# Top-k attention with a mixture of depths on one core: an exponential per head, bounds checked at the end, and the mixture's matmuls placed behind the turning of scores

## The chip, the core and the metric

One of the eight cores of a Trainium2 chip runs the whole program. The metric is the device time of one execution in microseconds (us). A core has engines that each work through a list of instructions in order: TensorE (PE in the profile, its weight loads PEld), VectorE (DVE), ScalarE (ACT), GpSimd (POOL), and SyncE (SP), which here only issues DMAs. They wait for one another through semaphores. PSUM, where TensorE writes, has banks of 512 f32 values per partition.

## What is computed

Batch 8, 8 heads, 576 positions, head dimension 64; every score row keeps its 32 largest entries.

```python
scores = scale * np.matmul(q, k.transpose(0, 1, 3, 2))
kth = np.partition(scores, -32, axis=-1)[..., -32:-31]
scores = np.where(scores >= kth, scores, -1e9)
attn = np.exp(scores - max);  attn = attn / (attn.sum(-1) + 1e-9)
x = (attn @ v) as (8, 576, 512)
# mixture of depths, for each batch b
s = x[b] @ w_gate
idx = the 128 positions of the largest s
out[b] = x[b];  out[b, idx] += sigmoid(s[idx]) * (relu(x[b, idx] @ w1) @ w2)
```

## The kernel before

The attention is cut into **units**: one pair of heads by one tile of 128 query rows (two pairs and the last 64 rows in the last tile). A batch has 18 units (`per_batch`), and there are `N` = 144. A unit passes through a pipeline that is written out by hand as one loop over steps `n`; the class `InOrder` keeps every engine's instructions in exactly the program's order. Nothing is planned by a scheduler. A unit m goes through these steps:

- `multiply` and `keep`: TensorE multiplies q by k into the PSUM tile `ps`, ScalarE copies it to `sc` (step m-1).
- `find_bound`: VectorE takes the eight largest of seven parts of each row (`cand`), then three rounds (`best`, `bound`) give a lower bound for the 32nd largest score (step m).
- `what_is_below`: ScalarE takes the sign of score minus bound (`sides`, counting into `seen`), GpSimd multiplies scores by signs into `y` (two instructions, one for each head) and `fill` adds a few values (step m+1).
- `kth_of`: VectorE finds the exact 32nd score (`next8`) as the eighth largest of `y` (step m+2).
- `mask_of`: `less` marks what is below it; head 0 on ScalarE, head 1 on GpSimd (step m+3).
- `weigh`, `values`, `keep_values`: TensorE transposes the scores and adds a large negative number where `less` is set (`turn`, into the PSUM tile `ptr`; one more 128 x 128 block, `turn_last`, goes to a corner of the bank `av`). ScalarE takes the exponential of both heads in one instruction (`pT`, 1024 columns from two banks) and of the corner (`last`). TensorE multiplies `pT` by v into `av`, and ScalarE copies the result to `xs` (step m+4).

Between these the program puts small work in by queues that are emptied at fixed points of a step: `late` (ScalarE, by `flush()` right after the mask), `vector_late` (VectorE, between the two heads of `find_bound`) and `pool_late` (GpSimd). A finished row tile is divided by its sums (`rden` on VectorE, `x` on GpSimd) and dotted with the gate weights (`prod` on VectorE).

The **mixture** of batch b runs while batch b+1 and the first half of b+2 are in the loop, cut into 25 pieces by a generator; `mix_steps` says after which step a piece comes. The first pieces store and reload the gates and count ranks; later ones fetch 128 rows, transpose them, and do one eighth of the first product (`multiply_h`, four matmuls into `h_ps`) or of the second (`y_ps`, one matmul). In the kernel before, the pieces of step n are issued at the very end of step n, so that on TensorE they stand behind `values` and ahead of the next step's `turn`.

`keep_least` is called once for each batch, behind `mask_of` of its last unit. On VectorE it takes the low 23 bits of all 36 bounds of the batch (`low`), and three minima into `least`: of the bounds, of the 32nd scores, and of `low`. At the end of the program these minima, `seen`, `sums`, `ranks` and `others` are reduced to one number per partition, `sure`; `count_unsure` sums it over partitions by a matmul on TensorE, and a general version of everything runs if a case was found that the fast way does not cover. It did not run here.

The last batch's mixture, `closing`, cannot hide behind other units. Its order on TensorE is: the rest of the y matmuls of the batch before (`between`), the transposes of the fetched rows `xe`, the matmul of `count_unsure`, then four blocks of `multiply_h` and the 8 matmuls of the second product.

Of the kernel before, what the change touches and what calls it, by code (L numbers as in the profile page):

```python
# [10 lines left out]
AF = mybir.ActivationFunctionType  # L11
# [20 lines left out]
J = 4  # L32
# [16 lines left out]
def kernel(  # L49
# [80 lines left out]

    NS = B * 2 * (J * NHP + NHP // 2)
    seen = const.tile([P, NS], FP32, name="seen")
    least = const.tile([P, 3, B], FP32, name="least")
    sums = const.tile([P, B * NT, H], FP32, name="sums")
    nc.gpsimd.memset(sums, 1.0)

# [50 lines left out]
    def flush():  # L187
        while late:
            late.pop(0)()
# [119 lines left out]
                    )  # L309

    def turn_pair(rows, hp, copy=None):
        tr = ps_tr.tile([P, 2, J, P], FP32, name="ptr")
        for w in range(2):
            rows.turn(2 * hp + w, tr[:, w, :, :])
        for w in range(2):
            rows.keep(2 * hp + w, tr[:, w, :, :], copy=copy)

    def turn_all_last(rows, copy=None):
        tr = ps_misc.tile([P, 2, 2, P], FP32, name="tr", tag="misc")
# [149 lines left out]
    def turn_some(tr, z, less):  # L469

        pe.transpose(tr, z, ident)
        if less is not None:
            pe.matmul(
                tr, less, out_of_reach, start=False, stop=True, skip_group_check=True
            )

    def room_to_turn():
        return ps_tr.tile([P, 2, J, P], FP32, name="ptr"), ps_av.tile(
            [P, 512], FP32, name="av"
        )  # L480

    def turn(z, tr, less=None):

        for i in range(2):
            for c in range(J):
                at = slice(c * P + i * R, (c + 1) * P + i * R)
                turn_some(
                    tr[:, i, c, :], z[:, i, at], None if less is None else less[:, i, at]
                )

    def turn_last(z, av, less=None):
# [11 lines left out]
    def values(t, g, pT, last, av, vs):  # L503

        vt, vpair = vs
        for i, heads in enumerate(heads_of(t, g)):
            for c in range(J):
                for r in (0, R):
                    h = heads[-1 if r else 0][0]
                    pe.matmul(
                        av[r : r + R, i * DE : (i + 1) * DE],
                        pT[:, i, c, r : r + R],
                        vt[:, h, c, :],
                        start=(c == 0 and i == 0),  # L520
                        stop=False,
                        skip_group_check=True,
                    )
# [222 lines left out]
    def closing(b, pg, between):  # L746
# [7 lines left out]
        pick = modpool.tile([P, NT, CAP], BF16, name="pick")  # L754

        def spread(t0, t1):
            tr = ps_tr.tile([P, 2, J, P], FP32, name="ptr")
            n = R if t0 == J else P
            for t in range(t0, t1):
                pe.transpose(  # L760
                    tr[:, 0, t - t0, 0:n],
                    gate[0:n, t : t + 1].to_broadcast([n, P]),
                    ident[0:n, 0:n],
                )
            act.copy(
                out=gate_row[:, t0 * P : (t1 - 1) * P + n].rearrange(
                    "p (t i) -> p t i", i=n
                ),
                in_=tr[:, 0, 0 : t1 - t0, 0:n],
            )  # L770

        def count(t, among, rank):
# [59 lines left out]
        dve.reciprocal(out=g, in_=g)  # L832

        xeT = modpool.tile([P, NDC, CAP], FP32, name="xeT")
        ps = ps_tr.tile([P, 2, J, P], FP32, name="ptr")[:, 0, :, :]
# [5 lines left out]
        for f0 in range(0, NFC, 2):  # L841
            h_ps = (
                lambda: room_for_scores()[:, 0, 0, :],
                lambda: ps_av.tile([P, 512], FP32, name="av"),
                lambda: ps_misc.tile([P, 512], FP32, name="h_ps", tag="misc"),
                lambda: ps_tr.tile([P, 2, J, P], FP32, name="ptr")[:, 0, :, :].rearrange(
                    "p c i -> p (c i)"
                ),
            )[f0 // 2 % 4]()
# [183 lines left out]
    def is_unit(n):  # L1033
        return 0 <= n < N

    def weigh(sc, tr, av, less):

        turn(sc, tr, less)
        tr_last = turn_last(sc, av, less)
        pT = ptpool.tile([P, 2, J, P], FP32, name="pT")  # L1040
        last = ptpool.tile([P, P], FP32, name="last")

        def exp():
            act.activation(pT, tr, AF.Exp, scale=scale)
            act.activation(last, tr_last, AF.Exp, scale=scale)

        return pT, last, exp
# [23 lines left out]
        find_kth(ys.pop(n), next8s[b][:, i, :, :])  # L1071

    def keep_least(b, bound, kth):
        low = stats.tile([P, per_batch, 2], I32, name="low", bufs=1)
        dve.tensor_scalar(
            out=low,
            in0=bound.bitcast(I32),
            scalar1=(1 << 23) - 1,
            scalar2=1,
            op0=ALU.bitwise_and,  # L1080
            op1=ALU.bitwise_xor,
        )
        for w, of in enumerate((bound, kth, low)):
            dve.tensor_reduce(
                out=least[:, w, b : b + 1], in_=of, axis=mybir.AxisListType.XY, op=ALU.min
            )

    def mask_of(n, on=None):
        b, i = divmod(n, per_batch)
        masks[n] = mask(scs[n], next8s[b][:, i, :, :], on)  # L1090
        if i == per_batch - 1 and b < B - 1:
            keep_least(b, bounds.pop(b)[:, :, :, 7], next8s.pop(b)[:, :, :, 7])

    for n in range(-1, N):
        b, i = divmod(n, per_batch)
# [25 lines left out]
        if is_unit(n - 4):  # L1121
            tr, av = room_to_turn()
            pT, last, exp = weigh(scs.pop(n - 4), tr, av, masks.pop(n - 4))
            exp()
        if is_unit(n - 3):
            mask_of(n - 3, (act, None) if n in scatter_steps else None)
        flush()
# [47 lines left out]
        if gating is not None:  # L1175
            b, t = gating
            if t == J:
                store(out[b], of_batch[b][0])
                mixtures[b] = mixture(float(b * S), of_batch[b][1], ranks[:, b, :])
        for b in mix_steps.get(n, ()):  # L1180
            next(mixtures[b], None)
        b, i = divmod(n, per_batch)
        if i == v_at and 0 <= b < B - 1:
            load_v(v[b + 1], qkv[b + 1][2])
# [2 lines left out]

    def other_room():
        ps = room_for_scores()
        return ps[:, 0, :, :].rearrange("p u (c i) -> p u c i", c=J), ps[:, 1, 0, :]  # L1190

    x, pg = of_batch[B - 1]
    between = mixtures[B - 2]
# [16 lines left out]
    def sums_of(t, xs):  # L1210
        n = R if t == J else P
        keep_sums(n, xs, sums[0:n, (B - 1) * NT + t, :])

    weigh_unit(N - 4)
    weighed[N - 4][2]()
    what_is_below(N - 1)
# [36 lines left out]


    keep_least(B - 1, bounds.pop(B - 1)[:, :, :, 7], next8s.pop(B - 1)[:, :, :, 7])
    sure = stats.tile([P, 1], FP32, name="sure")
    dve.memset(sure, 1.0)
    for what, op, than, limit in (
        (least[:, 0, :], ALU.min, ALU.is_gt, LEAST),
        (least[:, 1, :], ALU.min, ALU.is_gt, LEAST),  # L1260
        (least[:, 2, :], ALU.min, ALU.is_gt, 0.5),
        (seen, ALU.max, ALU.is_lt, float(MIDDLE)),
        (seen, ALU.min, ALU.is_gt, float(MIDDLE - 16)),
        (sums.rearrange("p t h -> p (t h)"), ALU.min, ALU.is_gt, FEWEST),
        (sums.rearrange("p t h -> p (t h)"), ALU.max, ALU.is_lt, MOST),
    ):
# [62 lines left out]
    def general(b, row0):  # L1329
# [11 lines left out]
        for t in range(NT):  # L1341
            xs = xpool.tile([P, H, DE], FP32, name="xs")
            for g in range(groups(t)):
                ps = room_for_scores()
                multiply(t, g, kT, qT, ps)
                p = general_weights(keep(ps))
                tr, av = room_to_turn()
                turn(p, tr)
                pT = ptpool.tile([P, 2, J, P], FP32, name="pT")
                last = ptpool.tile([P, P], FP32, name="last")  # L1350
                nc.scalar.copy(out=pT, in_=tr)
# [53 lines left out]
```

## Time and profile before

| | |
|---|---|
| median of 3 runs | 827.2 us (826.03 to 827.62) |
| the profiled execution: its own time, its span | 828.44 us, 826.1 us |
| VectorE busy | 787.2 us (95%) |
| TensorE busy | 777.0 us (94%) |
| ScalarE busy | 730.7 us (88%) |
| GpSimd busy | 715.4 us (87%) |
| mean granted TensorE clock | 0.990 |

The span runs from the first to the last instruction; all times inside the profile are counted from its start. Busy time is the union of an engine's instruction intervals, and neighbouring instructions overlap a little: a row's duration is longer than the distance from its start to the next start. In a group of instructions the columns are engine, operation, output<-inputs, shapes, count, then busy time and mean duration in nanoseconds, then the idle time before them and what ended it. Almost all instructions carry line 45, where `InOrder` records them, so they are told apart by tile names.

### The profile page before, as it was taken

The page shows a single profiled execution, that of the slowest core. Times are in us where ns is not written, and L with a number is a line of the kernel's source. Part 1 is how long each engine was busy: PE and PEld are TensorE (multiplying, and loading weights), DVE is VectorE, ACT ScalarE, POOL GpSimd, SP SyncE. Part 2 cuts the span into 40 slices and gives each one's busy share as a digit, 9 for nine tenths or more (in the row PEclk, how much of TensorE's full clock was granted, in tenths as well). Part 3 has the DMA queues.
Part 4 walks back from the last instruction along what each step waited for, and adds up shares of the span by engine and source line. Part 5 has one row for each costly group of instructions (what it writes and reads, how often), then busy time and mean ns, then how long its engine had stood idle before and what let it go on. Part 6 is the DMA issues. An engine that isn't in the chain of part 4 may idle for free. (4 is left out here: it accounts for less than half of the span.)

```text
span 826.1 us, 28252 instructions
## 1 busy us (share of the span) xinstructions
PE 777.0 (94%) x10143; PEld 596.5 (72%) x10143; DVE 787.2 (95%) x4651; ACT 730.7 (88%) x1557; POOL 715.4 (87%) x722
## 2 busy tenths in 40 slices
PE   6888888888999999999999999999999999999976
PEld 5566666666887778877787777877787777767744
DVE  7899999999999999999999999999999999999960
ACT  4799999999999999999999999999999999879831
POOL 3799999999899999999899999999999998899831
PEclk9699999999999999999999999999999999999999
DMA  7931111521141221521223221512215102101021
GB/s 170 283 86 40 28 66 28 105 53 27 60 92 36 53 40 59 112 47 34 79 47 86 53 40 60 104 23 54 40 59 112 28 15 66 23 12 18 2 71 30
DMA packets 122133, 50.38 MB, mean 61 GB/s; under 512 B 116417, under 2 KB 116417, under 8 KB 120961
## 3 DMA queue, kind: packets, MB, share of 16 engines
q1 hardware_dynamic: 118672, 43.91, 22.0%
q0 software_dynamic: 1728, 4.20, 2.8%
q8 instruction: 82, 1.34, 0.8%
q14 instruction: 67, 0.54, 0.3%
q10 hardware_dynamic: 1584, 0.39, 0.2%
HBM read 36.93 MB, written 11.55 MB: 59 GB/s over the span
## 5 line engine op out<-in xcount | busy, mean ns | idle before, releaser
L45 POOL TENSOR_TENSOR y<-sc,sides 128x576 f32<-128x576 f32 x288 | 365.1, 1289 | 57.0 <-ACT sides L45 54.3
L45 DVE MAX8 cand<-sc 128x8 f32<-128x82 f32 (+1 forms) x2016 | 314.0, 228 | 2.7 <-ACT sc L45 2.7
L45 POOL TENSOR_SCALAR less<-sc,next 128x576 bf16<-128x576 f32 x135 | 232.5, 1722 | 12.9 <-DVE next L45 10.0
L45 PE MATMUL ptr<-out_of_reach,less 128*128 128x128 bf16 x1136 | 205.3, 220 | 19.5 <-POOL less L45 19.4
L45 ACT ACTIVATE sides<-sc,bound 128x576 bf16<-128x576 f32 x288 | 223.0, 787 | 0.0
L45 PE MATMUL ptr<-ident,sc 128*128 128x128 f32 x1136 | 217.0, 282 | 0.0
L45 DVE MAX8 next<-y 128x8 f32<-128x584 f32 x288 | 204.4, 751 | 1.7 <-POOL y L45 1.6
L45 PEld LDWEIGHTS av<-v,pT 128*64 128x64 f32 x4544 | 144.1, 137 | 66.9 <-ACT last L45 63.2
L45 PE MATMUL ps<-kT,qT 64*128 64x288 f32 (+1 forms) x1280 | 182.0, 431 | 5.2 <-ACT qT L45 5.2
L45 PEld LDWEIGHTS ptr<-ident,sc 128*128 128x128 f32 x1136 | 161.3, 142 | 29.1 <-issue 17.4
L45 ACT ACTIVATE pT<-ptr 128x1024 f32<-128x1024 f32 x142 | 145.3, 1023 | 33.2 <-PE ptr L45 32.2
L45 PE MATMUL av<-v,pT 128*64 128x65 f32 x4544 | 163.7, 224 | 9.3 <-ACT last L45 8.5
L45 ACT COPY sc<-ps 128x1152 f32<-128x1152 f32 (+1 forms) x144 | 162.2, 1126 | 3.5 <-PE ps L45 3.5
L45 PEld LDWEIGHTS <-less 128*128 128x128 bf16 x1296 | 136.1, 106 | 39.2 <-POOL less L45 25.2
L45 PEld LDWEIGHTS ps<-kT,qT 64*128 64x128 f32 (+1 forms) x1280 | 100.2, 178 | 41.5 <-issue 21.2
L45 ACT ACTIVATE less<-sc,next 128x576 bf16<-128x576 f32 x143 | 111.2, 777 | 12.7 <-DVE next L45 10.8
L45 DVE MATCH_REPLACE8 cand<-best,cand 128x21 f32<-128x21 f32 (+1 forms) x576 | 99.0, 180 | 0.0
L45 DVE MAX8 best<-cand 128x8 f32<-128x21 f32 (+1 forms) x576 | 90.5, 190 | 0.0
L45 PE MATMUL h_ps<-xeT,w 128*128 128x128 f32 x464 | 65.8, 286 | 0.0
L45 PEld LDWEIGHTS h_ps<-xeT,w 128*128 128x128 f32 x464 | 55.8, 191 | 9.2 <-issue 5.8
L45 PE MATMUL y_ps<-w,hT 128*128 128x512 f32 x112 | 60.6, 636 | 0.0
L45 ACT ACTIVATION_READ_ACCUMULATOR sides<-sc,bound 128x1 f32 x288 | 59.9, 208 | 0.0
(133 smaller groups left out, 866.4 us busy)
## 6 DMA issues: line engine op xcount, KB each, us to landing
v<-in_v_dram SPq DMA_DIRECT2D x64, 128.0 KB, 4.2
out_dram<-x SPq DMA_DIRECT2D x8, 1024.0 KB, 3.9
rows<-in_k_dram SPq DMA_DIRECT2D x56, 128.0 KB, 2.9
rows<-in_q_dram SPq DMA_DIRECT2D x56, 128.0 KB, 3.1
w<-in_moe_w_dram SPq DMA_DIRECT2D x2, 2048.0 KB
gate_row<-row_dram SPq DMA_DIRECT2D x7, 288.0 KB, 4.4
w<-in_k_dram SPq DMA_DIRECT2D x8, 128.0 KB, 3.2
last<-in_k_dram SPq DMA_DIRECT2D x8, 128.0 KB, 4.0
```

What stands on the lines that cost most here:

```text
L45: return lambda *a, **kw: self._tc.keep_in_program_order(fn(*a, **kw))
```

## The change

1. **A bank and an exponential for each head.** The two-bank tile `ptr` becomes two one-bank tiles, and `pT` two tiles. The exponential of a unit is issued as two instructions of 512 columns, one for each head, and then `last` as before. The same one-bank tiles serve the turning of k and q at the start and the closing mixture.
2. **The bounds' bits at the end.** `keep_least` no longer forms `low` and two of its minima. ScalarE copies the 36 bounds of a batch to `bounded` (through `late`), and VectorE keeps only the minimum of the 32nd scores. At the end `low` is formed over all 288 bounds at once, and `bounded` and `low` are reduced there, ahead of `count_unsure`.
3. **The mixture's pieces one place later.** The pieces of step n are issued in step n+1, behind the turning and the exponentials and ahead of the mask. On TensorE they stand between `turn` and `multiply`. Side by side, the instruction lists of SP and GpSimd are the same in both kernels, apart from names; on VectorE only the instructions of item 2 and the order of a few small ones differ.

```diff
     def turn_pair(rows, hp, copy=None):
-        tr = ps_tr.tile([P, 2, J, P], FP32, name="ptr")
+        tr = [turn_bank(w) for w in range(2)]
         for w in range(2):
-            rows.turn(2 * hp + w, tr[:, w, :, :])
+            rows.turn(2 * hp + w, tr[w])
...
+    def turn_bank(i=0):
+        return ps_tr.tile([P, J, P], FP32, name=f"ptr{i}")
...
+    def room_for_weights():
+        return [ptpool.tile([P, J, P], FP32, name=f"pT{i}") for i in range(2)], ptpool.tile(
+            [P, P], FP32, name="last"
         )
...
         def exp():
-            act.activation(pT, tr, AF.Exp, scale=scale)
+            for i in range(2):
+                act.activation(pT[i], tr[i], AF.Exp, scale=scale)
             act.activation(last, tr_last, AF.Exp, scale=scale)
...
     def keep_least(b, bound, kth):
-        low = stats.tile([P, per_batch, 2], I32, name="low", bufs=1)
-        dve.tensor_scalar(
-            out=low,
-            in0=bound.bitcast(I32),
-            scalar1=(1 << 23) - 1,
-            scalar2=1,
-            op0=ALU.bitwise_and,
-            op1=ALU.bitwise_xor,
-        )
-        for w, of in enumerate((bound, kth, low)):
-            dve.tensor_reduce(
-                out=least[:, w, b : b + 1], in_=of, axis=mybir.AxisListType.XY, op=ALU.min
-            )
+        at = 2 * per_batch * b
+        late.append(
+            lambda: act.copy(
+                out=bounded[:, at : at + 2 * per_batch].rearrange("p (n i) -> p n i", i=2),
+                in_=bound,
+            )
+        )
+        dve.tensor_reduce(
+            out=least[:, b : b + 1], in_=kth, axis=mybir.AxisListType.XY, op=ALU.min
+        )
...
+    def mix(n):
+        for b in mix_steps.get(n, ()):
+            next(mixtures[b], None)
...
             pT, last, exp = weigh(scs.pop(n - 4), tr, av, masks.pop(n - 4))
             exp()
+        mix(n - 1)
         if is_unit(n - 3):
             mask_of(n - 3, (act, None) if n in scatter_steps else None)
         flush()
...
-        for b in mix_steps.get(n, ()):
-            next(mixtures[b], None)
...
+    mix(N - 1)
     weigh_unit(N - 4)
...
     keep_least(B - 1, bounds.pop(B - 1)[:, :, :, 7], next8s.pop(B - 1)[:, :, :, 7])
+    flush()
+    low = modpool.tile([P, S], I32, name="low", tag="scratch")[:, 0:NS]
+    dve.tensor_scalar(
+        out=low,
+        in0=bounded.bitcast(I32),
+        scalar1=(1 << 23) - 1,
+        scalar2=1,
+        op0=ALU.bitwise_and,
+        op1=ALU.bitwise_xor,
+    )
     for what, op, than, limit in (
-        (least[:, 0, :], ALU.min, ALU.is_gt, LEAST),
-        (least[:, 1, :], ALU.min, ALU.is_gt, LEAST),
-        (least[:, 2, :], ALU.min, ALU.is_gt, 0.5),
+        (bounded, ALU.min, ALU.is_gt, LEAST),
+        (least, ALU.min, ALU.is_gt, LEAST),
+        (low, ALU.min, ALU.is_gt, 0.5),
```

More of the change, by code (lines that the diff above doesn't have):

```diff
@@ L132 @@
     seen = const.tile([P, NS], FP32, name="seen")
-    least = const.tile([P, 3, B], FP32, name="least")
+    least = const.tile([P, B], FP32, name="least")
+    bounded = const.tile([P, NS], FP32, name="bounded")
     sums = const.tile([P, B * NT, H], FP32, name="sums")
@@ L311, in turn_pair @@
     def turn_pair(rows, hp, copy=None):
-        tr = ps_tr.tile([P, 2, J, P], FP32, name="ptr")
+        tr = [turn_bank(w) for w in range(2)]
         for w in range(2):
-            rows.turn(2 * hp + w, tr[:, w, :, :])
+            rows.turn(2 * hp + w, tr[w])
         for w in range(2):
-            rows.keep(2 * hp + w, tr[:, w, :, :], copy=copy)
+            rows.keep(2 * hp + w, tr[w], copy=copy)
     def turn_all_last(rows, copy=None):
@@ L475, in turn_some @@
             )
+    def turn_bank(i=0):
+        return ps_tr.tile([P, J, P], FP32, name=f"ptr{i}")
     def room_to_turn():
-        return ps_tr.tile([P, 2, J, P], FP32, name="ptr"), ps_av.tile(
-            [P, 512], FP32, name="av"
+        return [turn_bank(i) for i in range(2)], ps_av.tile([P, 512], FP32, name="av")
+    def room_for_weights():
+        return [ptpool.tile([P, J, P], FP32, name=f"pT{i}") for i in range(2)], ptpool.tile(
+            [P, P], FP32, name="last"
         )
@@ L487, in turn @@
                 turn_some(
-                    tr[:, i, c, :], z[:, i, at], None if less is None else less[:, i, at]
+                    tr[i][:, c, :], z[:, i, at], None if less is None else less[:, i, at]
                 )
@@ L517, in values @@
                         av[r : r + R, i * DE : (i + 1) * DE],
-                        pT[:, i, c, r : r + R],
+                        pT[i][:, c, r : r + R],
                         vt[:, h, c, :],
@@ L756, in spread @@
         def spread(t0, t1):
-            tr = ps_tr.tile([P, 2, J, P], FP32, name="ptr")
+            tr = turn_bank()
             n = R if t0 == J else P
@@ L760, in spread @@
                 pe.transpose(
-                    tr[:, 0, t - t0, 0:n],
+                    tr[:, t - t0, 0:n],
                     gate[0:n, t : t + 1].to_broadcast([n, P]),
@@ L768, in spread @@
                 ),
-                in_=tr[:, 0, 0 : t1 - t0, 0:n],
+                in_=tr[:, 0 : t1 - t0, 0:n],
             )
@@ L834, in closing @@
         xeT = modpool.tile([P, NDC, CAP], FP32, name="xeT")
-        ps = ps_tr.tile([P, 2, J, P], FP32, name="ptr")[:, 0, :, :]
+        ps = turn_bank()
         for dc in range(NDC):
@@ L845, in closing @@
                 lambda: ps_misc.tile([P, 512], FP32, name="h_ps", tag="misc"),
-                lambda: ps_tr.tile([P, 2, J, P], FP32, name="ptr")[:, 0, :, :].rearrange(
-                    "p c i -> p (c i)"
-                ),
+                lambda: turn_bank().rearrange("p c i -> p (c i)"),
             )[f0 // 2 % 4]()
@@ L1039, in weigh @@
         tr_last = turn_last(sc, av, less)
-        pT = ptpool.tile([P, 2, J, P], FP32, name="pT")
-        last = ptpool.tile([P, P], FP32, name="last")
+        pT, last = room_for_weights()
         def exp():
-            act.activation(pT, tr, AF.Exp, scale=scale)
+            for i in range(2):
+                act.activation(pT[i], tr[i], AF.Exp, scale=scale)
             act.activation(last, tr_last, AF.Exp, scale=scale)
@@ L1189, in other_room @@
         ps = room_for_scores()
-        return ps[:, 0, :, :].rearrange("p u (c i) -> p u c i", c=J), ps[:, 1, 0, :]
+        banks = [ps[:, 0, i, :].rearrange("p (c i) -> p c i", c=J) for i in range(2)]
+        return banks, ps[:, 1, 0, :]
     x, pg = of_batch[B - 1]
@@ L1348, in general @@
                 turn(p, tr)
-                pT = ptpool.tile([P, 2, J, P], FP32, name="pT")
-                last = ptpool.tile([P, P], FP32, name="last")
-                nc.scalar.copy(out=pT, in_=tr)
+                pT, last = room_for_weights()
+                for i in range(2):
+                    nc.scalar.copy(out=pT[i], in_=tr[i])
                 nc.scalar.copy(out=last, in_=turn_last(p, av))
```

## The prediction, made before the changed kernel ran

> **What bounds the kernel now.** I read the busy times first, then the stages in windows, then the list of waits, and last the timeline around the instructions that the change touches. The page's first line does not decide:
>
> ```profile
> PE 777.0 (94%) x10143; PEld 596.5 (72%) x10143; DVE 787.2 (95%) x4651; ACT 730.7 (88%) x1557; POOL 715.4 (87%) x722
> ```
>
> Windows over two whole batches do (length, then PE, PEld, DVE, ACT and POOL busy with counts, granted clock, DMA):
>
> ```profile
> 402.23:498.33 96.10, 94.94 (x1261) 73.60 (x1261) 95.99 (x577) 91.49 (x198) 88.55 (x88) 1.00 0.27 60
> 498.33:594.45 96.12, 94.93 (x1261) 73.57 (x1261) 96.01 (x577) 91.57 (x198) 88.55 (x88) 1.00 0.26 60
> ```
>
> VectorE is busy for 95.99 of 96.10 us: a batch takes as long as VectorE's list. From the waits between 80 and 776 us (total, times, longest):
>
> ```profile
> PEld av L45 <- ACT last L45: 59.6, 123, 1.3
> ACT pT L45 <- PE ptr L45: 28.7, 72, 1.2
> ```
>
> TensorE and ScalarE wait for each other, in a ring: exponential, values, mixture's piece, turning, exponential. In steps with a piece the exponentials start at 539.99, 545.30 and 550.60, a ring of 5.30 us; VectorE needs 96.1 / 18 = 5.34. The ring costs nothing today, but 18 rounds are 95.4 us, so it is the next limit.
>
> **Part 1: what VectorE loses from each batch.** The rows of `low`, and the timeline of VectorE and GpSimd at one of its places (start, duration):
>
> ```profile
> L45 DVE TENSOR_SCALAR low<-bound x8: 175/1060/1231, 113.2 to 800.9; 128x36 int32<-128x36 int32 x8
> ```
>
> ```profile
> 496.82 2.52 POOL L45 TENSOR_TENSOR y<-sc,sides 128x576 f32<-128x576 f32 x2 [0.85 <-ACT sides L45]
> 498.33 1.06 DVE L45 TENSOR_SCALAR low<-bound 128x36 int32<-128x36 int32 x1
> 499.31 0.21 DVE L45 TENSOR_REDUCE least<-bound 128x1 f32<-128x36 f32 x1
> 499.45 0.20 DVE L45 TENSOR_REDUCE least<-next 128x1 f32<-128x36 f32 x1
> 499.58 0.17 DVE L45 TENSOR_REDUCE least<-low 128x1 f32<-128x36 int32 x1
> 499.67 0.51 DVE L45 MAX8 cand<-sc 128x8 f32<-128x82 f32 x3
> 502.18 2.53 POOL L45 TENSOR_TENSOR y<-sc,sides 128x576 f32<-128x576 f32 x2
> 504.86 1.72 POOL L45 TENSOR_SCALAR less<-sc,next 128x576 bf16<-128x576 f32 x1
> 505.49 0.67 DVE L45 CUSTOM_DVE_ANT_0 prod<-x,wg 128x512 f32<-128x512 f32 x1
> ```
>
> 36 elements take 0.17 us alone and 1.06 here: `low` ends when GpSimd's second `y` ends. From 498.33 to 499.67 is 1.34 us; the reduction that stays needs 0.14 to 0.2. So 1.17 us go from each of six batches, and 0.3 from the first, where `low` took 0.17: 7.3 us in all. The eighth lies behind the loop.
>
> Not all of this is kept, since it is mostly waiting for GpSimd, and five `prod` in a batch wait for GpSimd too. They last 0.67 us free, and in this batch 0.67, 0.98, 0.89, 1.11 and 0.82. The `prod` at 505.49 would come 1.17 earlier, at 504.3, into the second `y`, which lasts to about 504.65. At 774.55 a `prod` that came into a second `y` went in at its end, so I charge 0.35 there; the later four I leave nearly as they are, but ScalarE, and so GpSimd, comes later against VectorE for some steps, which I charge at 0.2. Kept: 0.6 for each of six batches, 3.6, and 0.3: 3.9 us. Bounds: the `prod` at 130.00 waited 2.1 us through `y`, the small fill and the start of `less`; if all first ones do, more than 1.17 goes and nothing is kept. If phases shift the good way, 7.3 is kept, and even the 1.1 us that the `prod` wait now in a batch could shrink.
>
> The Trainium skill ("SBUF — State Buffer", section "SBUF: two separate sides") says that VectorE and GpSimd take that pair as an exclusive lock for a whole instruction, and that a VectorE operation with two SBUF inputs, as `prod` is, needs it against a GpSimd operation that reads SBUF. The rows agree in part: `prod` beside `less` runs freely once `less` is about 0.6 us old, which a lock for the whole 1.72 us would forbid; by the rule each `prod` beside `less` would cost over a microsecond more and the sum would keep nothing.
>
> **Part 2: the exponential per head.** From one start to the next the 1024-column exponential takes 0.92 us and the 128-column `last` 0.16: 0.85 ns a column, hence 0.49 for 512 and 0.98 for two, 0.06 more a unit. With the batch's copy of 36 bounds (0.2) ScalarE grows by 1.3 to 92.8 us, against VectorE's new 94.9: hidden, with 2.1 us to spare. The upper bound takes whole durations: 273 ns for 128 columns and 1023 for 1024 give 594 for 512, 0.17 more a unit, 94.6 a batch, and the cover is gone. In return the first exponential starts when head 0 is turned, some 0.7 us earlier, which is worth something only where ScalarE waits.
>
> TensorE gains less than the change suggests: in the instruction list its first value matmul still has the unit's only wait for ScalarE, so both heads wait for the last exponential.
>
> **Part 3: the mixture's piece.** It moves on TensorE from ahead of `turn` to behind it, at no cost in matmuls. Between turning and values now lie the piece (0.95), the k and q transposes (0.35) and `multiply` (1.1), longer than the exponentials, so the ring opens and TensorE is left with 5.0 to 5.1 us a step. The scores of a later unit come up to 1 us later; VectorE reads them 3.7 us after ScalarE's copy. ScalarE's copies of `h_ps` stand behind the mask and find them ready. The DMAs, GpSimd's slots, fetches and scatters that the pieces issue keep their places on SP and GpSimd. Worth zero alone; without it the 95.4 us ring would stop Part 1 at 0.7.
>
> **Part 4: the end.** This is where the change pays. The timeline of the closing:
>
> ```profile
> 800.49 3.70 PE L45 MATMUL y_ps<-w,hT 128*128 128x512 f32 x8
> 804.23 0.69 ACT L45 ACTIVATE gy<-y_ps,g 128x512 f32<-128x512 f32 x1 [2.98 <-PE y_ps L45]
> 804.86 0.63 PE L45 MATMUL ptr<-ident,xe 128*128 128x128 f32 x4 [0.66 <-DMA xe<-out_dram,row_i]
> 804.96 0.16 DVE L45 TENSOR_TENSOR sure<-sure,far 128x1 f32<-128x1 f32 x1
> 805.41 0.19 PE L45 MATMUL av<-ones,sure 128*1 128x1 f32 x2
> 806.16 2.05 PE L45 MATMUL ps<-xeT,w 128*128 128x128 f32 x16 [0.56 <-ACT xeT L45]
> ```
>
> Today the checks run on VectorE from 800.93 to 805.12, while TensorE does y matmuls, and are done 0.3 us before TensorE asks. In the changed lists the last copy to `bounded` stands on ScalarE behind `gy`, which waits for the y matmuls. It starts at 804.8 and ends at 805.0. VectorE waits for it with `low`, and behind `low` are queued all reductions. Their length: 3.74 us from 801.38 to 805.12 today, less two small pairs of 0.27 and plus two of 288 elements at 0.56 (the `seen` pairs), 4.32, and 0.4 for `low` itself. `sure` is ready at 809.8 in place of 805.12; TensorE's matmul waits for it, and behind that matmul the whole of `multiply_h`, which starts at 810.0 in place of 806.16: 3.8 us, nothing beside it. Bounds 3.4 to 4.2.
>
> TensorE then stands idle for 4.3 us, and the windows of one microsecond near the start (granted clock third from the end) show what a gap does:
>
> ```profile
> 20.00:21.00 1.00, 0.00 (x0) 0.00 (x0) 1.00 (x8) 1.00 (x4) 1.00 (x2) 1.00 0.77 174
> 21.00:22.00 1.00, 0.64 (x3) 0.51 (x5) 1.00 (x12) 0.30 (x1) 1.00 (x2) 0.50 0.75 172
> ...
> 34.00:35.00 1.00, 1.00 (x12) 0.29 (x12) 1.00 (x2) 0.12 (x1) 0.97 (x1) 0.68 1.03 403
> ```
>
> A gap of 2.0 us (19.3 to 21.4) brought the clock to 0.50, and it came back at 34.7, after some 4 us without a gap. The pairs of `turn` start 0.32 us apart there and 0.172 at full clock. If the closing's first 3 to 6 us run so, 46% of that is lost: 1.4 to 2.9, and I take 2.1. Bounds: nothing, and the whole 14.3 us at half clock, 12. Together the end costs 5.9 us.
>
> The Trainium skill ("TensorE: Matmul & The Clock Gate", section "Part 1: The HAM clock gate") gives free-running windows of about 3.4 us, one idle to halve the clock and one busy to restore it. By it a gap of 4.3 would halve the clock only in some alignments; the row above dropped after 2.0, and the sum goes by the row.
>
> **The rest.** From 776 to 790 the exponential of unit N-4 waits 1.61 us for the whole turning; head by head `sides` of the last unit comes 0.5 earlier, and VectorE's 1.35 us wait for `y` shrinks: 0.4 gained, less 0.06 for each of the last four exponentials, which stand on the path: 0.2 (0 to 0.8). At the start k's copy no longer waits for q's turning; between -0.3 and +0.6 gained, taken as 0.
>
> **Sum.** -3.9 - 0.2 + 5.9 = +1.8 us. The profiled execution (828.44, of which 826.1 are the span) would become 830.2. It lies 1.2 above the median of the runs, 827.2; from there I forecast 829.0.
>
> **The rivals.**
> - *The whole saving is kept* (faster). `prod` finds GpSimd's gaps; 7.3 + 0.2 in the last units + 0.3 at the start - 5.9 = 1.9 less: 825.3, or 823.2 if the clock holds as well. For it: `prod` at 505.49 runs free now. Against: it then lands inside `y`. With 0.5 from last units and start and 0.3 from the first batch, the sign turns at (5.9 - 0.5 - 0.3) / 6 = 0.85 us kept in each of the six others.
> - *The clock holds at the end*: 2.1 less, 826.9. For it: the gap comes once, after full work. Against: the row at 21.
> - *Nothing is kept*: ScalarE at the upper bound (94.6 of 94.9) or `prod` behind `less` takes it back: 827.2 + 5.9 - 0.2 = 832.9.
> - *The loop gets longer*: steps with two pieces of `multiply_h`, 1.8 us ahead of `multiply`, starve ScalarE and then VectorE: 835 and more. Against: VectorE's 3.7 us of reserve.
>
> **Chances.** The forecast 0.45 (own range 827.3 to 830.7), whole saving 0.22, clock holds 0.13, nothing kept 0.17, longer loop 0.03. About 0.2%, 1.65 us, can be told from no change: faster 0.25, same 0.28, slower 0.47. The range 823.8 to 833.6 leaves out the lowest part of the second case and the highest of the last two.
>
> **What would show it.** In the loop: VectorE still busy for all but 0.3 us of a batch of 95.3 to 95.7; ScalarE's wait for `ptr` under 10 us, and `prod` rows longer than now. At the end: `bounded` behind `gy`, `sure` some 4.5 us later, TensorE's first `ps<-xeT` waiting for VectorE, granted clock near 0.5 behind it. I am wrong if the checks are done before the y matmuls, if batches fall to 95.0 or below, or if VectorE waits for `sc` or `y` in the loop.

## The result

The changed kernel takes 838.55 us (median, 837.91 to 839.25) against 826.62 (825.6 to 827.62) for the kernel before on the same chip: 1.0145 times as long, 95% interval 1.0131 to 1.0158. The forecast was 829.0, with a range up to 833.6. The profiled execution has a span of 836.6 us, 10.5 more than before.

**The loop.** The page's first line, then the window of one whole batch (length, PE, PEld, DVE, ACT and POOL busy with counts, granted clock, DMA):

```profile
PE 782.8 (94%) x10143; PEld 596.8 (71%) x10143; DVE 794.8 (95%) x4628; ACT 737.8 (88%) x1709; POOL 727.5 (87%) x722
```

```profile
505.71:603.17 97.46, 95.75 (x1264) 73.34 (x1261) 97.32 (x574) 92.07 (x216) 90.70 (x88) 1.00 0.26 59
```

VectorE has three instructions fewer in this batch, and it is busy 1.3 us longer. The waits between 80 and 776 us (total, times, longest), first two lines of the kernel before, then the changed kernel:

```profile
PEld L45 <- POOL less L45: 19.7, 22, 1.4
PE ptr L45 <- POOL less L45: 15.5, 21, 1.3
```

```profile
PEld L45 <- POOL less L45: 33.3, 54, 1.4
PE ptr L45 <- POOL less L45: 24.0, 48, 1.2
PEld av L45 <- ACT last L45: 19.9, 41, 1.3
ACT qT L45 <- PE ps L45: 16.5, 37, 1.0
```

The exponentials hold TensorE up much less (19.9 us, 59.6 before): the ring that the prediction named has opened. In its place TensorE waits for GpSimd's `less` (24.0 us on PE, 15.5 before), and ScalarE for the turned q (`qT`), a wait that the list of before does not have. The timeline shows how the two belong together (start, duration; in brackets the idle time before and what ended it):

```profile
427.89 1.11 PE L45 MATMUL h_ps<-xeT,w 128*128 128x128 f32 x8
...
428.84 0.38 PE L45 MATMUL ps<-ident,rows 128*128 128x128 f32 x2
...
429.15 1.24 PE L45 MATMUL ps<-kT,qT 64*128 64x288 f32 x8
429.22 0.79 ACT L45 ACTIVATE less<-sc,next 128x576 bf16<-128x576 f32 x1
...
430.44 0.38 ACT L45 ACTIVATE qT<-ps 128x256 f32<-128x256 f32 x1 [0.44 <-PE ps L45]
...
430.72 1.11 ACT L45 COPY sc<-ps 128x1152 f32<-128x1152 f32 x1
...
431.74 0.27 ACT L45 COPY xs<-av 128x130 f32<-128x130 f32 x1
...
432.16 0.76 ACT L45 ACTIVATE sides<-sc,bound 128x576 bf16<-128x576 f32 x1
...
433.10 2.52 POOL L45 TENSOR_TENSOR y<-sc,sides 128x576 f32<-128x576 f32 x2 [0.94 <-ACT sides L45]
```

The piece (`h_ps`) now stands ahead of the q transposes and of `multiply`. ScalarE, done with its mask at 430.0, waits for them; behind `qT`, in ScalarE's order, stand `sc`, `xs` and then `sides`, although `sides` needs none of the three. GpSimd waits 0.94 us for `sides`; behind its `y` stand the fill and `less`, and for `less` TensorE waits when it turns head 1. The kernel before at a like place, ScalarE's mask first:

```profile
428.96 0.78 ACT L45 ACTIVATE less<-sc,next 128x576 bf16<-128x576 f32 x1
...
429.62 0.38 ACT L45 ACTIVATE qT<-ps 128x256 f32<-128x256 f32 x1
...
431.34 0.76 ACT L45 ACTIVATE sides<-sc,bound 128x576 bf16<-128x576 f32 x1
...
432.27 2.52 POOL L45 TENSOR_TENSOR y<-sc,sides 128x576 f32<-128x576 f32 x2 [0.25 <-ACT sides L45]
```

There `qT` waits for nothing, and `sides` starts 2.38 us after the mask in place of 2.94. Over four steady batches this distance is 2.35 us on average before and 2.76 in the changed kernel.

A second effect is in the same trace, between VectorE and GpSimd:

```profile
438.46 2.53 POOL L45 TENSOR_TENSOR y<-sc,sides 128x576 f32<-128x576 f32 x2
...
440.37 1.17 DVE L45 CUSTOM_DVE_ANT_0 prod<-x,wg 128x512 f32<-128x512 f32 x1
440.94 0.67 POOL L45 TENSOR_TENSOR y<-steps,seen 128x16 f32<-128x16 f32 x1
...
441.59 1.72 POOL L45 TENSOR_SCALAR less<-sc,next 128x576 bf16<-128x576 f32 x1
```

`prod` comes into GpSimd's second `y`, waits to its end and goes in ahead of the fill, which takes 0.67 us in place of 0.21. So GpSimd's `less` comes 0.45 later as well.

**The end** came as forecast: `bounded` behind `gy`, VectorE behind `bounded`, TensorE behind `sure`; then the clock (third from the end in the windows of 2 us):

```profile
808.03 0.69 ACT L45 ACTIVATE gy<-y_ps,g 128x512 f32<-128x512 f32 x1 [2.98 <-PE y_ps L45]
808.61 0.24 ACT L45 COPY bounded<-bound 128x36 f32<-128x36 f32 x1
...
808.89 0.31 DVE L45 TENSOR_SCALAR low<-bounded 128x288 int32<-128x288 int32 x1 [3.96 <-ACT bounded L45]
...
813.59 0.19 PE L45 MATMUL av<-ones,sure 128*1 128x1 f32 x2 [4.29 <-DVE g L45]
...
813.71 2.50 PE L45 MATMUL ps<-xeT,w 128*128 128x128 f32 x10
```

```profile
814.00:816.00 2.00, 2.00 (x10) 2.00 (x10) 0.00 (x0) 0.00 (x0) 0.00 (x0) 0.50 0.00 0
...
820.00:822.00 2.00, 2.00 (x20) 2.00 (x19) 0.00 (x0) 0.38 (x1) 0.00 (x0) 1.00 0.00 0
```

**Where the 10.5 us are.** From VectorE's first to its last maximum over `y` the loop takes 766.7 us, 762.9 before: the first two batches are 3.6 shorter, the rest 7.4 longer. From there to the end it is 47.5 us, 40.8 before: 6.7 more. The start gives 0.1 back. The first batch varies: 94.6 before, 92.1 here, 93.4 and 94.0 in two runs below that have the same code up to the end. So its 2.5 us are partly chance.

### The profile page after: what moved, and what is told of

It is laid out like the page before. It is cut to its first block, busy times and chain, and to the rows that moved or that the text cites. A ratio compares the mean times of both kernels' runs of the same rounds, so it can differ in the third digit from the quotient of the medians.

```text
span 836.6 us, 28352 instructions
## 1 busy us (share of the span) xinstructions
PE 782.8 (94%) x10143; PEld 596.8 (71%) x10143; DVE 794.8 (95%) x4628; ACT 737.8 (88%) x1709; POOL 727.5 (87%) x722
## 5 line engine op out<-in xcount | busy, mean ns | idle before, releaser
L45 PE MATMUL ptr<-ident,sc 128*128 128x128 f32 x1136 | 225.3, 285 | 0.0
L45 PEld LDWEIGHTS <-less 128*128 128x128 bf16 x1296 | 139.1, 109 | 42.9 <-POOL less L45 40.6
L45 ACT ACTIVATE pT<-ptr 128x512 f32<-128x512 f32 x284 | 152.9, 591 | 2.8 <-PE ptr L45 2.4
L45 PE MATMUL h_ps<-xeT,w 128*128 128x128 f32 x464 | 63.3, 281 | 0.0
L45 PE MATMUL y_ps<-w,hT 128*128 128x512 f32 x112 | 58.5, 617 | 0.0
L45 ACT ACTIVATION_READ_ACCUMULATOR sides<-sc,bound 128x1 f32 x288 | 56.5, 196 | 0.0
```

The source lines that it names most:

```text
L45: return lambda *a, **kw: self._tc.keep_in_program_order(fn(*a, **kw))
```

## The experiments

Two numbers are worked out for each run. The **batch** is the mean of four batches, from the 55th to the 127th step's maxima over `y`. **TensorE's waits** come from its timeline: for each pair of neighbouring groups (head 0's turning to the last tile's, `multiply` to values, and so on) the time from start to start, and what it is over the median of that pair by more than 0.05 us, summed over a batch. The batch less these waits is TensorE's own list; the split between the two is good to some 0.2 us. "Fill" is GpSimd's small fill, all 18 of a batch.

| run | median us | batch | own list | waits | for `less` | for exponential | fill |
|---|---|---|---|---|---|---|---|
| before | 826.3 to 827.7 | 96.10 | 94.2 | 1.9 | 0.1 | 1.2 | 3.9 |
| after | 838.55 | 97.47 | 94.1 | 3.4 | 2.9 | 0 | 6.7 |
| e1 piece back | 830.2 | 96.17 | 94.3 | 1.9 | 0.1 | 1.3 | 5.2 |
| e2 one exponential | 838.6 | 97.28 | 94.2 | 3.1 | 2.5 | 0.1 | 5.8 |
| e3 bits back | 830.1 | 96.87 | 94.3 | 2.5 | 1.3 | 0.7 | 3.9 |
| e4 prod later | 838.6 | 97.49 | 94.1 | 3.4 | 2.9 | 0 | 6.7 |
| g1 fill between | 837.55 | 97.44 | 94.0 | 3.5 | 2.9 | 0 | 4.3 |
| g2 work added to after | 841.8 | 97.59 | 94.2 | 3.4 | 2.8 | 0 | 6.7 |
| i1 work added to before | 831.9 | 97.05 | 94.3 | 2.8 | 0.2 | 2.0 | 3.9 |
| g6 prod behind fill | 838.4 | 96.74 | 94.3 | 2.5 | 1.4 | 0.6 | 4.0 |
| h1 matmul over `sure` in the middle | 834.4 | 97.52 | 94.1 | 3.4 | 2.9 | 0 | 6.7 |
| h3 piece behind multiply | 838.8 | 98.60 | 96.8 | 1.8 | 1.3 | 0 | 6.9 |
| k1 between heads | 824.95 | 96.12 | 94.2 | 1.9 | 0.1 | 1.2 | 5.2 |
| j1 sides early | 817.4 | 96.00 | 94.0 | 2.0 | 0 | 0 | 4.9 |

The last three rows are built on h1, and are to be compared with it and not with the row "after". In j1 1.2 us of TensorE's waits are for `xs`.

**One part undone at a time** (the end stays as in the changed kernel, except in the third):

```diff
 # e1_pieces_back: the piece at the end of the step, as before
-        mix(n - 1)
...
+        mix(n)
 # e2_one_exp: one tile of two banks, one instruction
-            for i in range(2):
-                act.activation(pT[i], tr[i], AF.Exp, scale=scale)
+            act.activation(pT.both, tr.both, AF.Exp, scale=scale)
 # e3_bits_back: low and its reductions in every batch, least[:, 0..2, :]
```

> The changed kernel with the mixture's piece back at the end of the step, ahead of the next turning; the exponential per head and the bits at the end stay. Theory T (the piece behind the turning stands ahead of the k and q transposes and of multiply, ScalarE's in-order copies kT, qT and sc wait for them, sides and y come some 1 us later against VectorE, and prod and pick run into GpSimd's second y): the batch falls from 97.4 us to 95.6 or below, ScalarE's 36 waits for ps ahead of qT (16.1 us) go, the end keeps its +6.6 and the start its -2.4, so 826 to 828 us. Rival A (two exponentials in place of one make ScalarE late): the batch stays at 97.4, 838 us. Rival B (low was the wait that held VectorE in phase with GpSimd, and without it the prods wait instead): the batch comes to 96.1 or above, 831 us or more. Rival C (the ring of TensorE, ScalarE and GpSimd sets the batch and VectorE's waits for the port only fill it): the ring is tighter again, about 95.4 to 97 us, no clear answer.

> The changed kernel with one exponential over both heads on one tile of two banks, as before the change; the piece stays behind the turning and the bits at the end. Theory T: batches stay at 97.4 us or rise a little, since one exponential makes the first value matmul no later; the start loses its 2.4 us, so 839 to 842 us. Rival A (the two exponentials make ScalarE late): batches fall to 95.5, so 827 to 830 us. Rival B: batches stay at 97.4. Rival C (ring): the single exponential starts when both heads are turned, the ring is longer, batches above 97.4.

> The changed kernel with low and its reductions back in every batch, as before the change; the exponential per head and the piece behind the turning stay. Theory T (the later y is what costs, and low only adds to VectorE's list): batches 97.4 to 98.6 us, the end costs nothing more (sure early again), so about 832 to 839 us. Rival B (low held VectorE in phase, without it prod and pick wait instead): batches back to 96.1, the end as before the change and the start 2.4 shorter, so 823 to 825 us. Rival A: batches 97.4 or above, as by T. Rival C (the ring sets the batch): batches stay at exactly 97.4 and the time falls by the end's 6.6 alone, to 832 us.

Measured: 830.2, 838.6 and 830.1 us. With the bits at the end the piece's place costs 8.4 us (9.2 by the ratios to the kernel before, 1.0145 and 1.0034); beside the moved piece the second exponential costs and brings nothing in the time (rival A falls). The bits back bring 8.5, of which the end is 6.6 by its rows, and the steady batch falls from 97.47 to 96.87 although VectorE gets about 1.2 us more to do: fills at 3.9 again, waits for `less` at 1.3. That is part of what rival B says. It also means that the place and the bits belong together: with the bits in every batch, the moved piece and the new exponentials took only 2.9 us more than the kernel before in the same round (830.1 against 827.25).

**Is VectorE the limit?**

```diff
 # e4_prod_later: held-back work behind both heads' maxima
-            if i == 1:
-                flush_vector()
...
+        flush_vector()
 # g2_max_added (after) and i1_before_max (before): work that nothing needs
             kth_of(n - 2)
+        if gating is not None and is_unit(n - 1):
+            spare = stats.tile([P, 8], FP32, name="spare")
+            dve.max(spare, scs[n - 1][:, 0, 0:256])
```

> The changed kernel with VectorE's held-back work (prod, pick and what else is queued there) behind the fourteen maxima of both heads in place of between the two heads: the same instructions, seven maxima (3.3 us) later. Theory T (the price is paid where VectorE's instructions with two inputs meet GpSimd's second y): prod falls into less in place of y, lasts 0.67 to 0.9 us in place of 0.96 to 1.51, and the batch falls to 96.0 or below, 828 to 831 us. Rival C (the ring of TensorE, ScalarE and GpSimd sets the batch): the batch stays at 97.4, VectorE has idle time in place of long prods, 838 us. Rival A and B say the same as T here as far as prod goes.

> The changed kernel with work added on VectorE that nothing needs: five times a batch, behind the maxima over y, one maximum over 256 columns (about 0.35 us), 1.75 us a batch. Theory T (VectorE's list sets the batch): the batch grows by up to 1.75 us, 97.5 to 99.2, 839 to 849. Theory C (VectorE is ahead of the ring of the other engines and only fills its time with waits): batch 97.4, 838 to 839. Theory D (VectorE comes too early and its prods go in ahead of GpSimd's fill): with VectorE later the fills fall back to 0.21 us, the batch to 96.8 or below, as with low put back, 831 to 835.

> The kernel before with work added on VectorE that nothing needs: five times a batch one maximum over 256 columns, 2.05 us a batch as the same addition measured in the changed kernel. If VectorE's list sets the batch of before (as the prediction said: busy 95.99 of 96.10), the batch grows to 98.1 and the time to about 841 us. If TensorE's list and its waits set it and VectorE's busy time holds waits for the port that shrink instead (the low at 1.06 in place of 0.17, the prods at 4.48 in place of 3.35 a batch, 2.0 in all), the batch stays within 0.4 of 96.1, 827 to 832 us with what the first two batches add.

The windows of one batch, of g2 and then of i1:

```profile
408.92:506.38 97.46, 95.73 (x1264) 73.37 (x1262) 97.32 (x580) 92.08 (x217) 90.72 (x88) 1.00 0.26 59
```

```profile
408.40:505.48 97.08, 95.06 (x1265) 73.57 (x1263) 96.97 (x583) 91.47 (x197) 88.44 (x88) 1.00 0.27 59
```

Each added maximum took 0.41 us, 2.05 a batch. In the changed kernel this batch stays at 97.46 us and VectorE's busy time at 97.32: the work went into time that VectorE had spent waiting for GpSimd, which the profile counts as busy (`prod`, `pick` and the one `less` a batch that VectorE does were together 1.5 us shorter a batch; `pick` marks the mixture's chosen rows). Of the 3.2 us that the run took longer, 2.4 and 1.0 are in the first two batches; by the ratios to the kernel before the two runs differ by 1.9 us, and the first batch varies by as much with the same code. The `prod` moved behind seven more maxima (1.1 us) ran into the same place of `y`: VectorE runs ahead of the others until it is held there, so the long rows of `prod` are slack on VectorE and no price there. In the kernel before, about half of the added work is hidden: the batch grew by 0.95 of 2.05. There VectorE counted, but it had about 1.1 us in reserve that "busy 95.99 of 96.10" hides.

**The fill.**

```diff
 # g1_fill_between: the fill between the two y
             part(i, sc, bound, at, sides)
+            if i == 1:
+                fill(y, at)
 # g6_prod_behind_fill: VectorE reads the fill before its held-back work (prod, pick, less)
             if i == 1:
+                if vector_late and filled is not None:
+                    dve.max(spare, filled[:, 0, S : S + 8])
                 flush_vector()
```

> The changed kernel with GpSimd's small fill put between the two y of a step in place of behind the second. Theory D (in the changed kernel VectorE comes early enough for prod, pick and less to wait through the second y and go in at its end, ahead of the fill, which then takes 0.66 us in place of 0.21; GpSimd's less and TensorE behind it come 0.45 later five or six times a batch, 2.8 us of GpSimd a batch): with the fill already done the batch falls to 95 to 96.2 us and the time to 827 to 831. Theory T (VectorE's own list, with its waits for the port, sets the batch): the prods still wait for the end of y, batch 97.2 to 97.5, 837 to 839. Rival C (a ring of TensorE, ScalarE and GpSimd sets it, whatever VectorE does): between the two; the fill's 2.8 us go from the ring as by D, unless the fill now waits for the second sides, then 97.4 or above.

> The changed kernel (its end included) with one small maximum on VectorE ahead of each prod that reads what GpSimd's fill wrote, so that prod always comes behind the fill and never holds it up. VectorE gets some 0.1 us and a wait more five times a batch. Theory D with C (the ring sets the batch, and each prod that goes in ahead of the fill makes the ring 0.45 longer, five a batch): the fills fall from 6.7 to some 4.4 us a batch, the batch from 97.5 to 95.3 to 96.5, so 825 to 833 us. C without D (the ring's tight part is elsewhere): batch 97.4, 838 to 839. T (VectorE's list sets it): the batch grows by what VectorE waits more, 97.6 to 99, 839 to 848.

With the fill out of the way the `less` behind `y` took 2.15 us in place of 1.72 where `prod` went in: the wait moved by one instruction, and the batch stayed (97.44). With `prod` forced behind the fill the batch fell by 0.73 us, as with the bits back; the time did not, because the first batch grew by 5.1 (97.2 against 92.1, or 3.2 to 3.8 against the 93.4 and 94.0 of the two runs named above). So of the 1.37 us that a batch lost, 0.7 came from `prod`, `pick` and VectorE's `less` going in ahead of GpSimd, and the other 0.6 stay when they do not.

**The end.**

```diff
 # f1_check_last, f4 (with the piece back): TensorE's matmul over sure behind the closing
     next(closed)
-    count_unsure()
     next(closed, None)
+    count_unsure()
 # h1_check_mid, h2 (with the piece back): between multiply_h and the last y matmuls
+        yield      # in closing, behind the loop over f0
...
     next(closed)
+    next(closed)
     count_unsure()
```

> The changed kernel with one thing moved at the end: TensorE's little matmul over sure, and VectorE's step behind it, come after the rest of the closing and not ahead of multiply_h. If the tail is read rightly (3.7 us of waiting for sure, then 2.9 us lost at half clock behind the gap), both go: 6.6 less, 832 us, with the granted clock near 1.00 from the first ps<-xeT on. If only the wait goes and the clock halves for another reason, 834.8. If the last copies merely wait for something else, 837 to 838. The loop is the same in all cases, batches of 97.4 us.

> The changed kernel with the piece back at the step's end and TensorE's matmul over sure behind the rest of the closing. The piece back alone gave 830.2 us; the end as read is worth 6.6 less, so 823.6 us, ahead of the kernel before by 3.6. If the end is worth only its 3.7 us of waiting, 826.5, no different from before.

> The changed kernel with TensorE's matmul over sure between multiply_h and the last y matmuls of the closing, in place of ahead of multiply_h. With that matmul behind the whole closing the closing's own rows were back at their old lengths (20.0 us from the last eight y_ps matmuls to gy, against 26.7), but 2.7 us came back as the read of unsure and the branch, which then stood last. Here unsure is ready long before the scatter: all 6.6 to 6.7 us of the end should go, 832 us; if the branch costs as much wherever the matmul stands, 834.7 again.

> The same end, with the mixture's piece back at the step's end: 830.2 less 6.6, 823.6 us, against 826.1 with the matmul over sure behind the closing. Batches of 96.1 to 96.2 us.

Measured: 834.7, 826.1, 834.4 and 825.2 us. From `gy` on ScalarE to `gy` on VectorE it is 16.3 us before, 22.95 after, 16.3 with the matmul last and 16.55 with it in the middle, at a clock of 1.00: both the wait and the half clock are gone. With the matmul last, 1.8 to 2.2 us come back behind it, since the scatter and the end then wait for `unsure`. In time 3.8 to 5.0 us go, not 6.6. The profiled execution of the changed kernel had the longest closing of the seven runs that have this end (21.8 to 22.95, mean 22.3), and in h1's profile the first batch and the steps behind the last whole one came out 2.2 us longer than there, with the same code.

**Other places for the piece.**

```diff
 # h3_mid_check_mid: between multiply and values
             scs[n + 1] = keep(ps, n == -1)
+        mix(n - 1)
+        flush()
 # k1_between_heads: between the turning of the two heads
         for i in range(2):
+            if i == 1 and between:
+                between()
             for c in range(J):
```

> The same end, with the mixture's piece between multiply and the value matmuls of a step. Ring theory (C: GpSimd's less, TensorE's turning, k and q transposes and multiply, ScalarE's copies and sides, GpSimd's y, fill and less take two steps; 10.9 us with the piece in it, 10.0 without, against VectorE's 10.4 to 10.7): the piece is out of that ring and also out of the one from the values to the exponential, so batches of 95.0 to 96.2 us, 817 to 823.6 us. If any place behind the turning costs as much (for instance since the values come later, and their copies xs on ScalarE with them), batches stay at 97 or above and the time near 830.

> The changed kernel with the check of sure mid-closing (834.4 so far) and the mixture's piece between the turning of head 0 and that of head 1 in place of behind both. GpSimd's less is asked for by head 1's turning alone, so the piece now covers it, while ScalarE's first exponential still runs beside the piece. If TensorE's list with its waits sets the batch, the waits for less (2.9 a batch) go nearly all, TensorE's own list stays at 94.1 to 94.8, and the batch falls to 95 to 96: 817 to 825 us. If k and q copies and sides, still behind the piece, make GpSimd later by the same amount, the waits stay and the batch is 96.7 to 97.5: 829 to 835 us.

h3 missed: 838.8 us, against 834.4 for h1. The piece is out of `multiply`'s way, but now the values stand behind it, and `xs` on ScalarE waits for them with `sides` still behind `xs` (waits of h3, 80 to 776 us):

```profile
ACT xs L45 <- PE av L45: 40.2, 75, 1.2
```

By the table that is the smaller part of the miss: TensorE's waits are no longer than in h1 (1.8 us), and its own list grew from 94.1 to 96.8 us, with the same matmuls in another order. k1 came to 824.95 us and a batch of 96.12: GpSimd's `less` is asked for by head 1 only, and the piece covers it (0.1 us of waits for `less` in place of 2.9).

**Sides ahead of the copies.** TensorE's order stays as changed; only ScalarE's is different.

```diff
 # j1 (after, matmul over sure in the middle), j2 (the same, piece back),
 # k2 (the same, piece between heads), l1 (the kernel before)
         flush()
+        if is_unit(n - 1):
+            find_sides(n - 1)      # the two part() of what_is_below
         if is_unit(n + 1):
             b, t, g = units[n + 1]
```

> The changed kernel with the check of sure mid-closing (834.4 us so far) and ScalarE's two sides put right behind its mask, ahead of the kT, qT and sc copies and of xs; TensorE's order stays. If TensorE's waits for less come by way of ScalarE (copies that wait for the transposes and multiply behind the piece, sides queued behind them, then GpSimd's y, fill, less), the sides come 2 us or more earlier, the waits for less fall from 2.9 us a batch to below 1.3 and the batch from 97.47 to 95 to 96.3: 818 to 827 us. If the late copies of sc make VectorE late instead, or GpSimd is late for another reason, the batch stays at 97 or above, 831 us and more.

> Both edits together: the piece between the heads' turning and the sides ahead of ScalarE's copies. By the theory of TensorE's list and its waits the batch comes to 94.6 to 95.5, VectorE's own list (93.9 us without its waits) then being next: 814 to 821 us. If sides early does harm (the sc copy comes 2 us later, VectorE has some 3 us in reserve), it is above the run with the piece between the heads alone.

> The kernel before with one reordering and nothing of the change: ScalarE's two sides right behind its mask, ahead of the kT, qT and sc copies and xs. In the changed kernel with the check mid-closing the same took 17.0 us off (834.4 to 817.4): 1.4 us a batch in the steady loop, 3 to 4.5 in each of the first three batches. If it is a gain of its own, 818 to 822 us here. If it only undoes what the piece's new place costs, 825 to 827: TensorE's waits in the loop of before are for the exponentials (1.2 us a batch), which sides early makes later rather than earlier.

> The changed kernel with the check mid-closing, sides early and the piece back at the step's end, against 817.4 us with the piece behind the turning. If the new place is worth something once sides no longer wait behind it (it takes away TensorE's waits for the exponential), 819 to 824 us here. If the place makes no difference then, 817 to 818. If the end of the step is the better place also then, 812 to 816.

The timeline of j1 at the like place:

```profile
419.67 0.78 ACT L45 ACTIVATE less<-sc,next 128x576 bf16<-128x576 f32 x1
...
420.33 0.77 ACT L45 ACTIVATE sides<-sc,bound 128x576 bf16<-128x576 f32 x1
...
421.28 2.52 POOL L45 TENSOR_TENSOR y<-sc,sides 128x576 f32<-128x576 f32 x2 [0.18 <-ACT sides L45]
...
421.85 0.37 ACT L45 ACTIVATE qT<-ps 128x256 f32<-128x256 f32 x1
```

`sides` begins 0.66 us after the mask began, 2.94 in the changed kernel above, and `qT` finds its transposes ready. Measured: j1 817.4, k2 817.4, j2 817.15 us: with `sides` early the piece's place moves the time by less than 0.3 us, where it moved it by 9.2 (834.4 against 825.2). That is the test of the theory: what the place costs is paid by what stands behind ScalarE's waiting copies. That the place itself costs nothing at all is not shown. The steady batches with `sides` early lie at 96.0 us, and those of the kernel before, e1 and k1 at 96.1 to 96.2; a small price could be hidden under whatever holds all of them there. With `sides` early TensorE no longer waits for `less` in these batches, but for ScalarE's `xs`, which now stands behind `sides` (waits of j1, 80 to 776 us):

```profile
PEld av L45 <- ACT xs L45: 21.8, 31, 1.0
PE av L45 <- ACT xs L45: 14.5, 29, 0.8
```

The reordering alone takes the kernel before to 822.4 us (ratio 0.9948, 0.9935 to 0.9962). Its gain is in the first two batches (89.1 and 94.4 us, 94.6 and 97.6 before); its steady batches are longer, 96.7 on average. With the change's exponentials and bits at the end, the matmul over `sure` in the middle and the piece back it is 817.15 (0.9888, 0.9873 to 0.9903), the lowest here, though not to be told from j1 and k2 (0.9897 both). Without the reordering the best were h2, 0.9976 (0.9963 to 0.9989), and k1, 0.9987 (0.9975 to 0.9998), which cannot be told apart.

## Why the prediction was wrong

- **The step that failed: Part 3, "at no cost ... Worth zero alone".** It measured 8.4 us (838.6 against 830.2), and 8.6 and 9.2 in the pairs with the other ends, all with the bits at the end; with the bits in every batch it was 2.9. The delay itself was seen ("The scores of a later unit come up to 1 us later"), and was set against VectorE, the reader of `sc`, with 3.7 us in reserve. The rest of ScalarE's list behind the copies was not followed: `sides`, and through GpSimd's `y` and `less` back to TensorE. "ScalarE's copies of `h_ps` ... find them ready" was true and beside the point; the copies of `ps` did not.
- **The case that came, "The loop gets longer: 835 and more", had 0.03.** Its place was right (ScalarE starved behind the piece), its price too. Its condition was not: it named steps with two pieces, and 88 of the 95 steps in which TensorE had such a product held one. Its victim was wrong as well: between 80 and 776 us the trace has no wait of VectorE for scores. TensorE waited.
- **"A batch takes as long as VectorE's list"** was read from busy time that holds waits for GpSimd. Added work showed the reserve: 1.1 us before, at least 1.9 after. TensorE's own list of 94.2 us was as near to the batch of 96.1 as VectorE's without its waits (94.0: 95.99 less 0.9 of `low` and 1.1 of `prod`).
- **Part 1, kept 3.9 us.** With the piece back (e1) the loop is 3.2 us shorter than before, though not 0.6 in each of six batches: 1.5 and 1.1 in the first two, 0.9 in the last steps, and nothing in the steady ones. Two more profiles of the same loop (f4 and h2) have 2.6 and 0.6 in place of 3.2, so the size is uncertain. In the steady batches the time of `low` turned into longer `prod`, VectorE's `less` and `pick` (0.6, 0.2 and 0.4 us a batch), as the rival of nothing kept has it. Beside the moved piece Part 1 was harmful: with VectorE earlier, `prod` went in ahead of the fill. The prediction charged VectorE 0.35 and 0.2 for such meetings and GpSimd nothing; GpSimd paid 2.8 us a batch in its fills in the changed kernel, and 1.3 in e1.
- **Part 2, nothing on the path:** right beside the moved piece, where e2 and the changed kernel agree within 0.1 us; with the piece back it was not tried alone. The first value matmul still waited for the last exponential.
- **Part 4, 5.9 us:** right. Seven runs with this end take 6.0 us longer from `gy` to `gy` than the kernel before (22.3 against 16.3); in the profiled execution it was 6.6, 3.7 of waiting and 2.9 of clock, where 2.1 was taken. The sum of all parts but the third is 829.0, since Part 3 stood in it with nothing; e1, which has all but Part 3, measured 830.2. That is near partly by luck, since Part 1's share did not come from the steady batches, as it should have.
- **The signs named ahead:** ScalarE's wait for `ptr` under 10 us (1.1), longer `prod` rows, `sure` 4.5 us later against `gy` (5.4 after its start, 0.9 before) and a clock of 0.50 all came. Batches of 95.3 to 95.7 did not.

Open: why the steady batches of j1, k2 and j2 stay near 96.0 us when their first three are 88.9, 94.4 and 94.9, and why those of l1 scatter from 95.3 to 98.0. TensorE's waits for `xs` are 1.2 to 1.5 us a batch in all four; no experiment took them away.

## What to carry to other kernels

When a block of work is moved on one engine, follow each copy that waits for it on the next engine to everything queued behind that copy, needed or not, and round the ring until it comes back; the reader of the copy is only one of those that pay. Before taking "busy all the time" for a limit, add a little work that nothing needs: if the time stays, the engine was waiting under another name. Where such a ring is found, look for instructions that stand late in an in-order list without needing what is ahead of them: putting `sides` first took 17.0 us off (h1 to j1), more than the piece's place had cost.

## What the runs showed of the hardware

The meeting of VectorE and GpSimd costs both sides. GpSimd's fill of 16 columns took 0.66 us behind a `prod` and 0.21 otherwise, its `less` 2.15 and 1.72 (g1), and the profile books all of it as busy. The Trainium skill ("SBUF — State Buffer", section "SBUF: two separate sides") says that of the two the one that starts first holds the shared ports and the other is blocked; the rows of `prod` behind `y`, and of the fill and `less` behind `prod`, agree. A `prod` that began 0.63 us or more after a `less` did not wait: in the kernel before it took its free 0.67 us there (505.49). In the changed kernel a `prod` that met a `y` went in ahead of GpSimd's next instruction in 33 of 34 cases. The other, at 127.45, met the end of one `y` and waited through the next one and the fill, 2.95 us in all.

TensorE takes different times for the same matmuls by their neighbours. Turning head 0 and head 1 took 1.37 us behind `h_ps` or `y_ps` and 1.42 directly behind the value matmuls; the four matmuls of one `multiply_h` took 0.95 us up to the transposes of k and q, 0.99 up to the turning and 1.09 up to the value matmuls. In h3 the list came out some 2.5 us a batch longer; why neighbours matter was not tested.
